# Windowed attention and two MLP layers on one core: the later plain pairs take q, scores and v another way, and ScalarE adds the 1e-9

## The chip, the core and the metric

The kernel runs on one core of a Trainium2 chip. The metric is the device time of one launch in microseconds; the median of three runs before the change is 904.41 us (902.61 to 905.0). The engines are TensorE (PE in the profile, its weight loads PEld), VectorE (DVE), ScalarE (ACT), GpSimd (POOL) and SyncE (SP), which here only issues DMAs.

## What is computed

Four batches of eight heads, 576 positions, 64 elements a head. Heads 0 to 3 are plain (a window of 32 positions back), heads 4 to 7 dilated (32 positions, each fourth one). Two MLP layers follow on the 2304 tokens.

```python
scores = scale * np.matmul(q, k.transpose(0, 1, 3, 2))
mask_plain = (rel >= 0) & (rel < window)
mask_dil = (rel >= 0) & (rel < window * dilation) & (rel % dilation == 0)
...
scores = np.where(masks[None, :, :, :], scores, -1000000000.0)
scores = scores - np.max(scores, axis=-1, keepdims=True)
attn = np.exp(scores)
attn = attn / (np.sum(attn, axis=-1, keepdims=True) + 1e-09)
return np.matmul(attn, v).astype(np.float32)
...
h = x @ w_in
g = np.maximum(0.01 * h, h)
return (g @ w_out).astype(np.float32)
...
h = x @ w_in
g = np.maximum(h, 0.0) + np.log1p(np.exp(-np.abs(h)))
return (g @ w_out).astype(np.float32)
```

## The kernel before

**Attention.** The tokens fall into eight windows of 288 (half a batch each, `w` 0 to 7), and in each window the heads into four pairs (`p` 0 to 3; 0 and 1 plain, 2 and 3 dilated): 32 pairs. A plain pair's window is cut into three tiles of 96 queries with 128 keys each, a dilated one into four of 72 queries, one for each residue. Scores stand with the keys in the partitions. The pairs of windows 0 and 1 are early: q and k are loaded in rows, transposed by TensorE, and the two heads' scores come as separate matmuls on 64 partitions each (`scores_early`, L603). The others are late: SP loads q and k in blocks of 32 by 32 (`load`, L523), VectorE transposes the blocks (`trans_k` L578, `trans_q` L585), and `trans_q` writes each head's q into its own half of a tile `qz` whose other half is zero, so that one matmul on 128 partitions gives the scores of both heads (`scores`, L630). VectorE adds the mask on the way out of PSUM (`mask`, L644), POOL takes the maximum over the partitions (`rowmax`, L654), VectorE subtracts it (L658), ScalarE takes the exponential (L661).

**Products with v.** In most pairs the exponentials are the stationary operand and v with a column of ones the moving one, so that the sums come along (`pv`, L679); VectorE adds 1e-9 to the sums, inverts them and multiplies (`inv`, L689 to L691), TensorE transposes the result (`xT`, L700). The dilated pairs from window 3 on (`turned`) keep v stationary: `pv_late` (L710) gives the result transposed at once, POOL sums the exponentials over the partitions (`sums`, L718), VectorE spreads, inverts and multiplies (L726 to L738). Both ways end in x, split into a high part by ScalarE (L757) and a low one by VectorE (L761).

**The MLPs.** Layer 1 takes the tokens in blocks (256, 256, 352, then 288 each) and the hidden units in 16 pieces `f`; a step is twelve matmuls `h` (L783), activation and split on ScalarE (L799, L804) and VectorE (`gl`, L808), and two steps later twelve matmuls `yp` (L826). Each of these stretches of twelve is called a group here. The first two blocks run interleaved. Layer 1's weights are converted ahead of the first products (low part by VectorE, L378). Layer 2's weights are converted piece by piece during layer 1 (L318 to L363) and stored to DRAM; layer 2 runs behind layer 1 with nothing of attention beside it. In the first 60 us, matmuls on constants (`spin`, L453) fill TensorE's idle time.

**What sets the order.** Every operation is an `Op` with an engine, an assumed cost, what it needs and frees, and a due time; `run_schedule` plays them through on assumed clocks and writes out one order for each engine. The engines then run in that order and wait for each other by semaphores. So a changed cost or due time anywhere can move rows on every engine. `C2A` and `C2B` set when layer 2's pieces are due; layer 1's chain of groups is fixed, and attention's work is put between the groups.

## Time and profile before

| | |
|---|---|
| runs, median (lowest to highest) | 904.41 us (902.61 to 905.0) |
| profiled execution, its own time | 903.69 us |
| its span, first to last instruction | 901.9 us |
| mean granted TensorE clock | 0.989 of full |
| busy PE, DVE, ACT, POOL | 98%, 71%, 44%, 13% |
| first product of layer 1 | 44.52 us |
| last of attention's low parts of x ends | 457.47 us |

The span is cut at the first and last instruction; a profile's times are from the span's start. A busy share is an average over stages with different limits: the first 60 us, layer 1 with attention between its groups (to about 505 us) and layer 2 are three of them. One matmul of 32-bit floats in attention shows as two records, and records overlap, so what a block costs is read from the starts of the matmuls ahead of it and behind it.

### The profile page before, as it was taken

To read this page: it belongs to the slowest core of one execution; us is meant where nothing else is said; L and a number is where in the kernel's file an instruction comes from. 1 tells how busy PE (TensorE), PEld (TensorE's weight loads), DVE (VectorE), ACT (ScalarE), POOL (GpSimd) and SP (SyncE) were. 2 spreads that over 40 slices of the span, in tenths; PEclk is the share of its full clock that TensorE was granted. 3 is DMA by queue.
4 is the path that set the end of the run, shared out by engine and by line. 5 is a ranking of instruction groups with operands and counts; after the bars stand their busy time and mean duration, and the time that the engine had idled before them with its cause. 6 is when DMAs were issued, how large, how long until landed. Compare 5 with 4: busy or idle time off the path is not lost.

```text
span 901.9 us, 16361 instructions
## 1 busy us (share of the span) xinstructions
PE 882.0 (98%) x6391; PEld 831.8 (92%) x6392; DVE 640.5 (71%) x1165; ACT 397.3 (44%) x763; POOL 112.8 (13%) x67
## 2 busy tenths in 40 slices
PE   6989999999999999999999999999999999999998
PEld 4879999999999999999999999988888888888886
DVE  3989996588688787786853675766765776576663
ACT  3767764444445444444435653323422432243231
POOL 5400021032042240221400000000000000000000
PEclk9879999999999999999999999999999999999999
DMA  9879124554565546554248477433443352325332
GB/s 237 220 212 312 21 36 98 168 133 120 139 176 173 139 124 173 156 156 158 72 148 292 136 222 236 149 94 101 162 143 109 112 170 94 107 104 156 103 94 93
DMA packets 157985, 131.89 MB, mean 146 GB/s; under 512 B 102100, under 2 KB 138964, under 8 KB 157908
## 3 DMA queue, kind: packets, MB, share of 16 engines
q1 hardware_dynamic: 155508, 130.26, 48.8%
q8 instruction: 50, 0.82, 0.4%
q10 hardware_dynamic: 2400, 0.59, 0.4%
q14 instruction: 27, 0.22, 0.1%
HBM read 104.60 MB, written 26.21 MB: 145 GB/s over the span
## 4 chain that ended last, share of the span: by engine, by line
PE 93%; DVE 1%; DMA 1%; ACT 0%; SPq 0%; issue 0%; DVEq 0%
PE yo L1032 22%; PE h L783 22%; PE yp L826 22%; PE h L959 17%; PE sc L630 3%; PE hp L1020 2%; PE pv L679 2%; PE pv L710 1%; PE xt L700 1%; DMA w2s<-cs 1%; DMA raw<-in_moe_w_out_dram 0%; PE sc L603 0%; DVE cf L336 0%; SPq L523 0%; DVE lent L658 0%
## 5 line engine op out<-in xcount | busy, mean ns | idle before, releaser
L783 PE MATMUL h<-xh,w 128*128 128x288 f32 (+2 forms) x1024 | 231.3, 301 | 1.2 <-DVE w L378 1.2
L826 PE MATMUL yp<-gh,w 128*128 128x288 f32 (+2 forms) x1024 | 229.4, 299 | 1.0 <-DVE ys L836 0.9
L1032 PE MATMUL yo<-wo,w 128*128 128x512 f32 x864 | 222.9, 395 | 0.0
L959 PEld LDWEIGHTS h<-tr,w 128*128 128x128 f32 x1344 | 174.3, 188 | 11.1
L1032 PEld LDWEIGHTS yo<-wo,w 128*128 128x128 f32 x864 | 152.5, 188 | 27.1
L959 PE MATMUL h<-tr,w 128*128 128x256 f32 x1344 | 176.7, 279 | 0.0
L783 PEld LDWEIGHTS h<-xh,w 128*128 128x128 f32 x1024 | 173.0, 190 | 1.9 <-DVE w L378 1.4
L826 PEld LDWEIGHTS yp<-gh,w 128*128 128x128 f32 x1024 | 171.7, 188 | 1.7 <-DVE ys L836 1.5
L783 PE MATMUL h<-xl,w 128*128 128x288 f32 (+2 forms) x512 | 152.0, 297 | 0.0
L826 PE MATMUL yp<-gl,w 128*128 128x288 f32 (+2 forms) x512 | 150.9, 295 | 0.0
L799 ACT ACTIVATE hc<-h 128x288 f32<-128x288 f32 (+2 forms) x128 | 52.4, 410 | 162.0 <-PE h L783 160.2
L997 ACT ACTIVATE ex<-ex 128x512 f32<-128x512 f32 x72 | 45.5, 632 | 154.8 <-DVE ex L994 154.7
L808 DVE TENSOR_TENSOR gl<-hc,gh 128x288 fp32r<-128x288 f32 (+2 forms) x128 | 68.0, 532 | 41.9 <-ACT gh L804 40.8
L783 PEld LDWEIGHTS h<-xl,w 128*128 128x128 f32 x512 | 97.3, 190 | 0.0
L826 PEld LDWEIGHTS yp<-gl,w 128*128 128x128 f32 x512 | 96.3, 188 | 0.2
L654 POOL PARTITION_ALL_REDUCE mx<-s x24 | 50.6, 2107 | 297.7 <-DVE s L644 294.0
L1000 DVE SCALAR_TENSOR_TENSOR ex<-hs,ex 128x512 f32<-128x512 f32 x64 | 44.3, 692 | 34.7 <-ACT ex L997 34.0
L1005 ACT ACTIVATE w<-ex 128x512 fp32r<-128x512 f32 x72 | 45.3, 629 | 33.0 <-DVE ex L1000 33.0
L804 ACT ACTIVATE gh<-hc 128x288 fp32r<-128x288 f32 (+2 forms) x128 | 56.6, 443 | 2.9
L1009 DVE TENSOR_TENSOR w<-ex,w 128x512 fp32r<-128x512 f32 x72 | 49.8, 691 | 11.5 <-ACT w L1005 6.5
L318 ACT ACTIVATE cf<-raw 128x512 f32<-128x512 f32 (+1 forms) x48 | 39.8, 830 | 22.4 <-DMA raw<-in_moe_w_out_dram 9.7
L336 DVE CUSTOM_DVE_ANT_0 cf<-raw,cf 128x1024 uint16<-128x1024 uint16 (+1 forms) x48 | 44.8, 933 | 1.0
(103 smaller groups left out, 964.7 us busy)
## 6 DMA issues: line engine op xcount, KB each, us to landing
wo<-w2o SPq DMA_DIRECT2D x80, 512.0 KB
raw<-in_moe_w_in_dram SPq DMA_DIRECT2D x32, 512.0 KB
raw<-in_moe_w_out_dram SPq DMA_DIRECT2D x32, 512.0 KB
w2o<-cf SPq DMA_DIRECT2D x16, 512.0 KB
out_dram<-o SPq DMA_DIRECT2D x36, 128.0 KB
w2a<-cf SPq DMA_DIRECT2D x8, 512.0 KB
w2s<-cs SPq DMA_DIRECT2D x8, 512.0 KB
w<-w2a SPq DMA_DIRECT2D x8, 512.0 KB
```

What stands on the lines that cost most here:

```text
L336: nc.vector.tensor_tensor(out=self.cf, in0=self.cf, in1=self.raw[:, :, 0], op=ALU.add)
L654: nc.gpsimd.partition_all_reduce(self.mx, self.sf, channels=P, reduce_op=bass_isa.ReduceOp.max)
L783: nc.tensor.matmul(out=h, lhsT=a[:, c, :], rhs=b_[:, c, :], start=(c == 0 and a is whi and b_ is xh), stop=(c == NC - 1 and a is wlo))
L799: nc.scalar.activation(out=hc, in_=hbank.pop(s), func=AF.Prelu, alpha=0.01)
L804: nc.scalar.activation(out=gh, in_=hcopy[s], func=AF.Copy)
L808: eng.tensor_sub(out=gl, in0=hcopy.pop(s), in1=gparts[s][0].bitcast(F32))
L826: nc.tensor.matmul(out=ybank[e][:, o:o + n], lhsT=a[:, e * P:(e + 1) * P], rhs=b_, start=(f == 0 and n == unit_len[u] and a is whi and b_ ...
L959: nc.tensor.matmul(out=bank[m, b][:, half], lhsT=w[:, a, kb * P:(kb + 1) * P], rhs=t[:, b_, kb], start=(kb == 0 and a + b_ == 0), stop=(kb ...
L997: nc.scalar.activation(out=self.ex, in_=self.ex, func=AF.Softplus)
L1005: nc.scalar.activation(out=self.gh, in_=self.ex, func=AF.Copy)
L1009: nc.vector.tensor_sub(out=self.gl, in0=self.ex, in1=self.gh.bitcast(F32))
L1032: nc.tensor.matmul(out=obank[c, t], lhsT=a, rhs=b_, start=(opens and n == 0), stop=(closes and n == 2))
```

## The change

Four things are changed, and the planner's numbers with them.

- Plain late pairs: `trans_q` transposes q in place, both heads in one instruction on 128 partitions, and `scores_plain` takes six matmuls on 64 partitions each, the heads alternating between the two halves, into two PSUM tiles; `mask_plain` masks head by head, with the masks in 16 bits.
- The sum of 1e-9 is made by ScalarE (`inv_sum`), for all pairs that are not turned; `inv` then only inverts and multiplies.
- The first pair (`p` 0) of windows 4 to 7 is turned: v stays stationary, POOL sums.
- The due times of layer 2's pieces: 110 us and 14 us a piece up to the sixth, then 26 us a piece, where it was 125 us and 19.9 us a piece throughout.

```diff
-            self.turned = w >= TURN and self.dil
+            self.turned = w >= TURN and (self.dil or w > TURN and p == 0)
...
         def trans_q(self):
+            if not self.dil:
+                self.qt = self.qr.rearrange("x n p -> x (n p)")
+                nc.vector.transpose(out=self.qt, in_=self.qr)
+                return
...
+        def scores_plain(self):
+            m = self.m
+            self.s = att.tile([P, self.nt, 2, m], F32, tag="s", name="s")
+            self.sc = [ps_a.tile([P, self.nt, m], F32, tag="at", name="sc") for j in range(2)]
+            for i in range(self.nt):
+                for j in range(2):
+                    hd = slice(D * j, D * j + D)
+                    nc.tensor.matmul(
+                        out=self.sc[j][:, i],
+                        lhsT=self.kt[hd, self.step * i:self.step * i + P],
+                        rhs=self.qt[hd, m * i:m * i + m],
+                        start=True, stop=True)
+
+        def mask_plain(self, j):
+            mk = masks_b if self.first else masks_b[:, 1:2].to_broadcast([P, self.nt, self.m])
+            nc.vector.tensor_tensor(out=self.s[:, :, j], in0=self.sc[j], in1=mk, op=ALU.add)
...
+        def inv_sum(self, half):
+            t0, t1, ps = self.po[half]
+            n, m = t1 - t0, self.m
+            self.rd[half] = rd = att.tile([m, n, 2, 1], F32, tag="rd", name="rd")
+            nc.scalar.activation(out=rd, in_=ps[:, :, :, D:D + 1], func=AF.Identity, bias=tiny[0:m])
...
-            rd = att.tile([m, n, 2, 1], F32, tag="rd", name="rd")
-            nc.vector.tensor_scalar_add(out=rd, in0=ps[:, :, :, D:D + 1], scalar1=1e-9)
+            rd = self.rd[half]
             nc.vector.reciprocal(out=rd, in_=rd)
...
-    C2A, C2B = 125.0, 19.9
+    C2A, C2B, C2N, C2C = 110.0, 14.0, 6, 26.0
...
-                tq = [Op("dve", 1.0 if turned else 1.2, a.trans_q, deps=[a.lq] + old_kq, rel=["qr"], lock=LOCKT, **m)]
+                tq = [Op("dve", (1.0 if turned else 1.2) if dil else 0.48, a.trans_q, deps=[a.lq] + (old_kq if dil else []),
+                         rel=["qr"] if dil else [], lock=LOCKT, **m)]
...
+            elif not dil:
+                a.o_s1 = Op("pe", 0.84, a.scores_plain, deps=[tk] + tq, acq=["at", "at", tag_s], rel=["qr"],
+                            order=[prev(1, "o_s1")], **ms)
+                cs = [Op("dve", dve(3 * a.m, True), a.mask_plain, j, deps=[a.o_s1], rel=["at"], hold=hold, **m) for j in range(2)]
...
-                norms.append(Op("dve", 0.8 if dil else 0.95, a.inv, half, deps=[pv],
-                                acq=["rd"], rel=[a.room(half if dil else p)[1], "rd"], **m))
+                sm = Op("act", 0.2, a.inv_sum, half, deps=[pv], acq=["rd"], **m)
+                norms.append(Op("dve", 0.63 if dil else 0.78, a.inv, half, deps=[sm],
+                                rel=[a.room(half if dil else p)[1], "rd"], **m))
...
-        c2 = C2A + C2B * (f + (which or 0) / 2)
+        c2 = f + (which or 0) / 2
+        c2 = C2A + C2B * min(c2, C2N) + C2C * max(c2 - C2N, 0.0)
```

**Where rows move.** First VectorE in the first 35 us, before the change: the third and fourth of the early pairs' subtractions of the maximum (`lent`), the first two normalisations (`rd`, `xn`) and the next step of a layer-1 piece (`cp`, L323).

```order
L658 TENSOR_TENSOR lent<-lent 128x576
L689 TENSOR_SCALAR rd<-pv 96x6
L690 RECIPROCAL rd<-rd 96x6
L691 TENSOR_TENSOR xn<-pv,rd 96x384
L658 TENSOR_TENSOR lent<-lent 128x576
L689 TENSOR_SCALAR rd<-pv 96x6
L690 RECIPROCAL rd<-rd 96x6
L691 TENSOR_TENSOR xn<-pv,rd 96x384
L323 TENSOR_SCALAR cp<-cf 128x1024
```

The same place on VectorE in the change:

```order
L677 TENSOR_TENSOR lent<-lent 128x576
L714 RECIPROCAL rd<-rd 96x6
L715 TENSOR_TENSOR xn<-pv,rd 96x384
L677 TENSOR_TENSOR lent<-lent 128x576
L714 RECIPROCAL rd<-rd 96x6
L715 TENSOR_TENSOR xn<-pv,rd 96x384
L677 TENSOR_TENSOR lent<-lent 128x576
L323 TENSOR_SCALAR cp<-cf 128x1024
```

The adds are gone, and the fifth subtraction stands ahead of the layer-1 piece. ScalarE at that place in the change (`lent<-sc` copies scores out, `lent<-lent` is the exponential, `rd<-pv,warm` the new sum, `cf<-raw` the second layer-1 piece's first step):

```order
L569 ACTIVATE lent<-tr 128x288
L708 ACTIVATE rd<-pv,warm 96x6
L622 ACTIVATE lent<-sc 128x288 x2
L680 ACTIVATE lent<-lent 128x576
L708 ACTIVATE rd<-pv,warm 96x6
L318 ACTIVATE cf<-raw 128x1024
```

Before, `cf<-raw` stood right behind the first of these rows; it is now behind two sums, two copies and an exponential. In the stretch up to the end of the early pairs TensorE also has 51 matmuls on constants where it had 42.

Second, TensorE in window 4 before the change: the first pair's products with v and the second pair's scores.

```order
L826 MATMUL yp_3028<-gh,w 128x288
L679 MATMUL pv<-v_94,s 96x65 x6
L630 MATMUL sc<-qz_91,kt_93 128x192 x2
L783 MATMUL h<-xh,w 128x288
...
L783 MATMUL h<-xh,w 128x288
L630 MATMUL sc<-qz_91,kt_93 128x192
L700 MATMUL xt<-ident,xn 128x96 x3
L826 MATMUL yp_3005<-gh,w 128x288
```

In the change the first pair's products are these, and the second pair's scores follow four groups later in one block of six:

```order
L734 MATMUL pv<-s,v_95 64x96 x6
L850 MATMUL yp_3062<-gh,w 128x288
...
L807 MATMUL h<-xh,w 128x288
L648 MATMUL sc<-qr,kt_94 128x96 x6
L850 MATMUL yp_3062<-gh,w 128x288
```

The transposes of that pair are gone. Counted in groups of twelve, the last pair's products with v of windows 4, 5, 6 and 7 stand at groups 123, 155, 187 and 219, before the change at 122, 154, 186 and 216; the next block of layer 1 begins behind groups 126, 158, 190 and 222 in both.

Third, VectorE where layer 1 goes from its second to its third block (`gl` is the low part of a step's activations, the others are layer 2's conversion, `ys` copies out of PSUM), before the change:

```order
L808 TENSOR_TENSOR gl<-hc,gh 128x256
L323 TENSOR_SCALAR cp<-cf 128x512
L327 SCALAR_TENSOR_TENSOR cf<-cf,cp 128x512
L336 ISA cf<-raw,cf 128x1024
L808 TENSOR_TENSOR gl<-hc,gh 128x256 x2
L808 TENSOR_TENSOR gl<-hc,gh 128x352
```

The same place in the change:

```order
L832 TENSOR_TENSOR gl<-hc,gh 128x256
L323 TENSOR_SCALAR cp<-cf 128x512
L327 SCALAR_TENSOR_TENSOR cf<-cf,cp 128x512
L336 ISA cf<-raw,cf 128x1024
L346 TENSOR_TENSOR cs<-cf 128x256
L832 TENSOR_TENSOR gl<-hc,gh 128x256
L346 TENSOR_TENSOR cs<-cs,cf 128x256
L346 TENSOR_TENSOR cs<-cf 128x256
L346 TENSOR_TENSOR cs<-cf,cs 128x256
L832 TENSOR_TENSOR gl<-hc,gh 128x352
```

A piece's sums (L346), which came some five steps later, stand here now. Between the 30th and the 52nd `gl` four pieces' last step (L363) stood before, seven do now; from there on they are about seven steps apart.

## Rows read from the trace of the kernel before

**Rows 1.** The page, part 1: busy us, share of the span, instructions.

```profile
PE 882.0 (98%) x6391; PEld 831.8 (92%) x6392; DVE 640.5 (71%) x1165; ACT 397.3 (44%) x763; POOL 112.8 (13%) x67
```

**Rows 2.** Windows of 10 us: length, busy PE, PEld, DVE, ACT, POOL, clock, DMA, GB/s.

```profile
40.00:50.00 10.00, 8.15 (x89) 7.13 (x86) 9.59 (x21) 7.01 (x17) 2.96 (x2) 1.00 0.60 129
50.00:60.00 10.00, 7.90 (x43) 7.69 (x44) 7.55 (x18) 7.83 (x12) 0.00 (x0) 0.50 0.67 163
...
150.00:160.00 10.00, 10.00 (x79) 10.00 (x79) 2.60 (x7) 4.09 (x10) 0.00 (x0) 1.00 0.38 84
...
210.00:220.00 10.00, 10.00 (x75) 9.70 (x74) 9.09 (x17) 3.41 (x7) 4.25 (x2) 1.00 0.30 85
```

**Rows 3.** Timeline of TensorE: start, duration, then idle before and its releaser.

```profile
48.03 1.58 PE L679 MATMUL pv<-lent 104*72 104x65 f32 x16 [1.61 <-ACT lent L661]
...
51.08 0.80 PE L783 MATMUL h<-xh,w 128*128 128x256 f32 x2 [1.19 <-DVE w L378]
...
234.11 0.40 PE L826 MATMUL yp<-gh,w 128*128 128x288 f32 x1 [0.94 <-DVE ys L836]
```

**Rows 4.** The chain that ended last, two groups: start, duration.

```profile
56.30 2.67 PE h L783 x12
...
62.72 1.40 PE h L783 x12
```

**Rows 5.** Timeline of TensorE around a plain pair's products and transposes (window 5).

```profile
362.43 0.29 PE L783 MATMUL h<-xh,w 128*128 128x288 f32 x1
362.56 1.15 PE L679 MATMUL pv<-v,s 128*96 128x65 f32 x12
...
363.74 0.29 PE L826 MATMUL yp<-gl,w 128*128 128x288 f32 x1
...
367.00 0.30 PE L783 MATMUL h<-xh,w 128*128 128x288 f32 x1
367.13 0.41 PE L700 MATMUL xt<-ident,xn 96*128 96x96 f32 x3
...
367.54 0.29 PE L826 MATMUL yp<-gl,w 128*128 128x288 f32 x1
```

**Rows 6.** Timeline of TensorE around a plain pair's scores, undivided.

```profile
353.06 0.29 PE L826 MATMUL yp<-gh,w 128*128 128x288 f32 x1
353.19 1.14 PE L630 MATMUL sc<-qz,kt 128*128 128x192 f32 x6
...
354.30 0.29 PE L826 MATMUL yp<-gl,w 128*128 128x288 f32 x1
```

**Rows 7.** Timeline of TensorE around a dilated pair's products, v stationary.

```profile
276.42 0.29 PE L826 MATMUL yp<-gh,w 128*128 128x288 f32 x1
276.64 0.72 PE L710 MATMUL pv<-s,v 104*64 104x72 f32 x16
...
277.53 0.30 PE L783 MATMUL h<-xl,w 128*128 128x288 f32 x1
```

**Rows 8.** Timeline of TensorE around an early plain pair's scores.

```profile
25.26 0.91 PE L603 MATMUL sc<-lent 64*128 64x96 f32 x12
26.10 0.54 PE L453 MATMUL spin<-masksb,identb 128*128 128x288 bf16 x3
```

**Rows 9.** Groups by line and form: busy us, mean ns, idle before.

```profile
L585 DVE STREAM_TRANSPOSE qz<-qr 64x288 f32<-64x288 f32 x48 | 28.4, 592 | 0.7
...
L689 DVE TENSOR_SCALAR rd<-pv 96x6 f32<-96x6 f32 x16 | 2.5, 157 | 5.3 <-PE pv L679 5.2
...
L757 ACT ACTIVATE xh<-xt 128x64 fp32r<-128x64 f32 x4 | 0.9, 216 | 0.0
```

**Rows 10.** Timeline of VectorE, then TensorE, where window 4's x is wanted.

```profile
281.49 0.69 DVE L761 TENSOR_TENSOR xl<-xn,xh 128x288 fp32r<-128x288 f32 x1
...
282.20 0.30 PE L826 MATMUL yp<-gh,w 128*128 128x288 f32 x1
...
283.80 0.30 PE L783 MATMUL h<-xh,w 128*128 128x288 f32 x1
```

More of the change, by code (lines that the diff above doesn't have):

```diff
@@ L387 @@
     masks_b = attp.tile([P, NI, QP], BF16, tag="masksb", name="masksb")
+    tiny = attp.tile([P, 1], F32, tag="warm", name="warm")
     zero = attp.tile([P, 1], BF16, tag="zero", name="zero")
@@ L435, in warm_up @@
     def warm_up():
-        t = attp.tile([P, 1], F32, tag="warm", name="warm")
         nc.gpsimd.partition_all_reduce(
-            t, ident[:, 0:1], channels=P, reduce_op=bass_isa.ReduceOp.max)
+            tiny, ident[:, 0:1], channels=P, reduce_op=bass_isa.ReduceOp.max)
+        nc.gpsimd.memset(tiny, 1e-9)
     BLOCKS = [(0, 256), (256, 256), (512, 352)] + [(t, T1) for t in range(3 * T1, NT, T1)]
@@ L638, in mask @@
             n, m = t1 - t0, self.m
-            if self.first and not self.dil and half == 0:
-                mk = masks[:, 0:2]
-            else:
-                sel = 0 if (self.first and self.dil) else 1
-                mk = masks[:, sel:sel + 1, 0:m].to_broadcast([P, n, m])
+            sel = 0 if self.first else 1
+            mk = masks[:, sel:sel + 1, 0:m].to_broadcast([P, n, m])
             nc.vector.tensor_tensor(
@@ L672, in pv @@
                 self.xn = att.tile([m, self.nt, 2, D], F32, tag="xn", name="xn")
-                self.po = {}
+                self.po, self.rd = {}, {}
             pool, tag = self.room(half if self.dil else self.p)
@@ L1180 @@
                         y_free[2 * (p % 2) + j].append(cs[j])
+            elif not dil:
+                a.o_s1 = Op("pe", 0.84, a.scores_plain, deps=[tk] + tq, acq=["at", "at", tag_s], rel=["qr"],
+                            order=[prev(1, "o_s1")], **ms)
+                cs = [Op("dve", dve(3 * a.m, True), a.mask_plain, j, deps=[a.o_s1], rel=["at"], hold=hold, **m) for j in range(2)]
             else:
-                blk = 0.33 if not dil else 0.29 if w < TURN else 0.2
+                blk = 0.29 if w < TURN else 0.2
                 s0 = Op("pe", 2 * blk, a.scores, 0, deps=[tk] + tq, acq=["at", tag_s],
```

## The prediction

> **What bounds the kernel now.** I read the page's shares first: TensorE is busy 98% of the span [rows 1]. Then the busy time by stretches of 10 us: from 60 us on TensorE has no idle time worth naming, while VectorE swings between 2.60 us of 10 (150 to 160) and 9.09 (210 to 220) [rows 2]. Then I went through TensorE's timeline from 62 us on and looked for steps between two matmuls longer than usual. Beside the attention blocks I found one real wait, 0.94 us at 234 us for a VectorE copy out of PSUM [rows 3]. So from 62 us on time is what TensorE has to do, and an edit pays by what it takes off TensorE, or costs by a wait that it makes there. Ahead of 62 us the picture is another: TensorE waits for the exponentials and for the converted weights (1.61 and 1.19 us) [rows 3], VectorE is at 9.59 of 10 from 40 to 50 us, and from 50 to 60 us the granted clock is 0.50, the lower level of 1.2 GHz, behind those waits [rows 2]. There VectorE's chain bounds, and the clock doubles what TensorE does: a group of twelve products takes 2.67 us at 56 us and 1.40 us at 63 us [rows 4].
>
> **What the blocks cost now.** An ordinary step is (283.80 - 282.20) / 12 = 0.133 us [rows 10]. The price of a block put into this stream is the distance from the last matmul ahead of it to the second behind it, less two steps of 0.133; the second, since the first behind a block often stands longer. A plain pair's products with v: 363.74 - 362.43 - 0.27 = 1.04 us; its three transposes: 367.54 - 367.00 - 0.27 = 0.27 [rows 5]. Scores of a plain pair: 354.30 - 353.06 - 0.27 = 0.97 [rows 6]. A dilated pair with v stationary (16 records of 72 columns): 277.53 - 276.42 - 0.27 = 0.84 [rows 7].
>
> **Change, part by part.**
>
> v stationary in four plain pairs (windows 4 to 7, first pair). Removed from TensorE: 1.04 + 0.27 = 1.31 us each. Added: 12 records of 96 columns. By records they cost 12/16 of 0.84 = 0.63, by columns (12 x 96 against 16 x 72, equal) 0.84. I take the middle, 0.74: gain 0.57 each, **2.3 us** for four (1.9 to 2.7).
>
> Scores in halves of the rows, twelve later plain pairs. The early pairs do this already, with the same twelve records of 64 rows and 96 columns: 26.10 - 25.26 = 0.84 us from their start to the next block's [rows 8]. What a change to halves costs on entry shows in the column halves: 276.64 - 276.42 = 0.22 where a step is 0.133, so 0.09 [rows 7]. The block then costs 0.84 to 0.93; I take 0.89 against 0.97: **1.0 us** for twelve (0.5 to 1.6). The masks stay 576 elements a pair. The Trainium skill, TensorEngine Tiling (Array Packing), Theoretical Speedup, gives up to twofold for a contraction of 64. By that rule the part would come to 5.8 us; the early pairs' blocks do not agree with it (0.84 for the records that would then take 0.49).
>
> q transposed in place: one instruction of 288 in place of two of 592 ns each [rows 9]; it was timed on 64 partitions, and the count of elements in a partition is unchanged. Twelve times 0.59 is 7.1 us off VectorE. Behind 62 us VectorE ends one wait of TensorE, so I price it at nothing; if VectorE is what is late (rival 4) it is relief. The q buffer is now held until the scores are done, so a later q load waits longer in SP's queue, and with it the k and v loads and layer-2 pieces behind; there are two such buffers, no wait of TensorE goes back to a load of q, and I take nothing.
>
> 1e-9 on ScalarE: 28 VectorE adds of about 0.157 us [rows 9] leave before, 24 small ScalarE operations come, and four pairs go to the other path, which has its own add. A ScalarE operation on 6 elements is not in the trace: under the 0.216 of 64 elements [rows 9], and I put it above the 0.157 of VectorE; take 0.2. Eight of the adds stand ahead of the second pair of layer-1 weights on VectorE, the instruction that the 1.19 us wait was for: 8 x 0.157 = 1.2 us earlier at best. ScalarE is in order and was at 7.01 of 10 there [rows 2], so a sum that waits for its products now holds back the exponentials and weight copies queued behind it, 8 x 0.2 = 1.6 us at worst. TensorE also gets nine more of the idle-time matmuls (51 for 42), 9 x 0.133 = 1.2 us if they meet real work. The new path is one engine longer, products, ScalarE, VectorE, but the step changes place with one of about its length. I take **0.8 us** gained, bounds 2.0 gained (1.2, and half of the 1.27 by which the group at 56 us is slower than the one at 63) and 2.8 lost (1.6 and 1.2).
>
> Four more sum reductions on POOL, and the longer VectorE tail of that path in place of the short one: TensorE does not wait for POOL anywhere behind 62 us, and what VectorE gets here is less than the sums and transposes take off it. Nothing, as long as VectorE keeps up (rival 4).
>
> The later x. In window 4 the last pair's x is done at 281.49 + 0.69 = 282.18 and TensorE wants it at 283.80: 1.62 us to spare [rows 10]. In the new order that pair's products with v stand three groups of twelve ahead of the wanted step, before it was four, and a group is 1.60 us; in windows 5 and 6 the same, in window 7 three for six. If the chain behind the products keeps its length, the spare time is zero. I charge **0.4 us** in all, bounds 0 and 3 (0.7 at each of four edges).
>
> Conversion dates of layer 2. Seven in place of four pieces end between the 30th and the 52nd step of layer 1, then they thin out. They fall where VectorE had 7.4 us of 10 free (150 to 160) and where it had 0.9 (210 to 220) [rows 2]. The one wait of 0.94 us there may go or get company: nothing, with 0.9 either way. The last piece's store comes later by one or two steps of layer 1, with some thirteen steps left; nothing.
>
> **The sum.** -2.3 - 1.0 - 0.8 + 0.4 = -3.7 us. The profiled execution took 903.69 us (span 901.9 and 1.8 around it), which lies inside the three runs (902.61 to 905.0) and 0.7 under their median. From the one 900.0, from the other 900.7: I say 900.5. A change of under 0.3%, 2.7 us, can hardly be told from none here.
>
> **The rivals.**
>
> 1. The forecast, 900.5, own range 898.8 to 902.3. For it: no waits to hide behind from 62 us on. Chance 0.50, of which 0.40 under 901.7.
>
> 2. What TensorE saves it waits away: x arrives late at the edges of the four blocks behind windows 4 to 7 (0.7 us each), so 2.8 of the 3.7 go: 903.3. For it: spare time near zero. Against: a place in the order counts whole groups, so up to a group of the shift may be rounding. Chance 0.17.
>
> 3. The change of halves costs on both sides of twelve blocks. By rows: 0.84 + 0.09 on entry + 0.13 for the longer first step behind a block (rows 6 hold one, 0.97 against 0.84) = 1.06, which is 0.09 more than now, 1.1 us lost where 1.0 was gained: 902.6. The Trainium skill, TensorEngine Tiling (Array Packing), Key Properties, states that changing the tiling mode drains TensorE; by that rule this is the case that comes. The 0.22 us entry agrees in kind. Chance 0.07.
>
> 4. Slower: layer-2 conversions crowd VectorE between 190 and 260 us, and the low parts of layer 1's activations come late behind them. Each such wait costs what the one at 234 us did, 0.94 [rows 3]. From four of them on the gain is gone, with seven it is 900.5 + 6.6 = 907. For it: 9.09 of 10 before any is added. Against: 0.59 us a plain pair and 0.157 a sum leave VectorE [rows 9], and a low part has two steps until it is used. Chance 0.13.
>
> 5. Better: TensorE keeps 2.4 GHz in the start-up, since the nine added idle-time matmuls sit where it waited. Two groups at 2.67 become 1.40: 2.5 us more, and no wait at the edges (0.4): 897.6. Against: the waits of 1 to 2 us that came ahead of the fall stay in kind. Chance 0.11. Halves that overlap fully would make a block of scores half of 0.97, 5.8 us off in place of 1.0, 895.7; against it stand the 0.84 us of the early blocks [rows 8]. Chance 0.02.
>
> **From cases to numbers.** Faster by over 0.3%: 0.40 + 0.13 = 0.53. Within: 0.10 + 0.17 + 0.07 = 0.34. Slower: 0.13. The range from 896.8 to 905.2 takes in the bounds of the terms and leaves out most of case 4 and the full overlap, under 0.2.
>
> **What would show it.** Right: the plain block with v stationary inserted at 0.6 to 0.85 us and no transposes in those pairs; the halved scores at 0.84 to 0.93; the second weights' low part some 1 us ahead of 51 us; no new waits of TensorE behind 62 us. Wrong: waits of TensorE on x at the first product of a block or on the copies out of PSUM; a stretch at clock 0.50 longer than 10 us ahead of 62 us; halved scores over 1.0 us.

## The result and the profile after

The changed kernel takes 908.28 us (median of 20 runs, 903.77 to 919.5) where the kernel before takes 903.11 in the same session (20 runs, 901.76 to 905.0). The ratio is 1.0062, with an interval of 1.004 to 1.0084: slower, by more than 0.3%, where I had said 900.5 and a range up to 905.2. One run, the 919.5, fell into a disturbed state and is left out of the ratio. The profiled execution took 904.88 us, with a span of 902.7, so it is one of the shorter ones.

The page of the changed kernel, part 1, answers to [rows 1]: TensorE is as busy as before, VectorE is less so.

```profile
PE 883.3 (98%) x6460; PEld 827.0 (92%) x6461; DVE 628.6 (70%) x1141; ACT 399.6 (44%) x787; POOL 126.0 (14%) x72
```

What changed is the chain that ended last (part 4). In the kernel before it is 93% TensorE, 1% DMA and 1% VectorE.

```profile
PE 88%; DMA 5%; DVE 4%; issue 1%; ACT 1%; SPq 1%; POOL 0%; ACTq 0%; DVEq 0%
```

The windows of the changed kernel answer to [rows 2], with two more.

```profile
40.00:50.00 10.00, 7.99 (x87) 7.05 (x86) 9.44 (x17) 7.80 (x17) 3.15 (x2) 1.00 1.01 237
50.00:60.00 10.00, 8.82 (x67) 8.12 (x67) 9.36 (x20) 8.24 (x15) 0.00 (x0) 0.83 0.54 103
150.00:160.00 10.00, 10.00 (x77) 10.00 (x76) 4.37 (x10) 5.20 (x11) 0.00 (x0) 1.00 0.78 251
160.00:170.00 10.00, 9.42 (x65) 8.81 (x64) 8.47 (x15) 3.45 (x8) 1.96 (x1) 1.00 0.70 220
180.00:190.00 10.00, 7.87 (x59) 7.51 (x58) 3.92 (x8) 4.59 (x10) 0.00 (x0) 1.00 0.74 244
210.00:220.00 10.00, 10.00 (x75) 9.70 (x74) 9.48 (x16) 4.22 (x8) 5.28 (x2) 1.00 0.22 62
```

From 180 to 190 us TensorE lacks 2.13 us, and VectorE is busy for only 3.92 us of the ten. So VectorE is not crowded there; it waits itself. TensorE's waits of the changed kernel from 80 us on are these (total, times, longest), where the kernel before has the 0.94 us of [rows 3] alone (one more, new as well, lies ahead of 80 us: 1.27 us at 62.77 for a low part of x; it comes back in the part on the 1e-9 below):

```profile
PE sc L648 <- ACT gh L828: 2.1, 1, 2.1
PE yp L850 <- DVE ys L860: 2.0, 2, 1.4
```

VectorE's waits between 100 and 260 us for the store of `cs` (2.7, once, in the kernel before):

```profile
DVE cp L323 <- DMA w2s<-cs: 10.6, 3, 5.1
```

The timelines of VectorE, ScalarE, SyncE's queue and TensorE in the changed kernel tell how the 2.13 us came about.

```profile
179.82 0.52 DVE L832 TENSOR_TENSOR gl<-hc,gh 128x352 fp32r<-128x352 f32 x1
185.48 0.43 DVE L323 TENSOR_SCALAR cp<-cf 128x512 uint32<-128x512 uint32 x1 [5.14 <-DMA w2s<-cs]
...
188.14 0.69 DVE L363 TENSOR_TENSOR cf<-cf 128x512 fp32r<-128x512 f32 x1 [0.26 <-ACT cf L360]
188.75 0.18 DVE L714 RECIPROCAL rd<-rd 96x6 f32<-96x6 f32 x1
189.03 0.55 DVE L715 TENSOR_TENSOR xn<-pv,rd 96x384 f32<-96x384 f32 x1
```

```profile
182.91 0.67 ACT L318 ACTIVATE cf<-raw 128x512 f32<-128x512 f32 x1 [3.45 <-DMA raw<-in_moe_w_out_dram]
...
187.48 0.63 ACT L360 ACTIVATE cf<-cf 128x512 fp32r<-128x512 f32 x1 [2.47 <-DVE cf L336]
188.02 0.25 ACT L708 ACTIVATE rd<-pv,warm 96x6 f32<-96x6 f32 x1
```

```profile
179.93 0.33 SPq L356 DMA_DIRECT2D w2s<-cs  x1
```

```profile
182.11 1.15 PE L698 MATMUL pv<-v,s 128*96 128x65 f32 x12
...
187.09 0.46 PE L648 MATMUL sc<-qr,kt 64*128 64x96 f32 x2
189.69 0.88 PE L648 MATMUL sc<-qr,kt 64*128 64x96 f32 x10 [2.13 <-ACT gh L828]
```

Read it from the store. `cs`, the column sums of a pair of layer-2 pieces, lies in the same single buffer as `cp`, the shifted word of the next piece. The store of `cs` is issued at 179.93, and VectorE's next instruction in order wants that buffer: it stands from 180.34 to 185.48. Not all of this is the store's: the instruction also reads `cf`, the piece's first step on ScalarE, which waited for the piece's load and ended only at 183.58. The last 1.9 us are the store's alone. The conversion then runs late, ScalarE stands 2.47 us for it, and behind that stands the new 1e-9 step of a plain pair whose products with v were done at 183.3. The reciprocal and the product that free that pair's PSUM bank end at 189.58, and at 189.69 TensorE, which needs a second bank for the halved scores, goes on. The profile names ScalarE's `gh` as the releaser, since it ended at the same time (189.55); the bank fits the order better, and the record of TensorE's sequencer that waits there on VectorE's semaphore (and on a DMA's) ends at 189.63. The two waits on `ys`, which end at 162.24 and 236.95, come behind such stands too:

```profile
159.71 0.43 DVE L323 TENSOR_SCALAR cp<-cf 128x512 uint32<-128x512 uint32 x1 [2.62 <-DMA w2s<-cs]
...
227.79 0.43 DVE L323 TENSOR_SCALAR cp<-cf 128x512 uint32<-128x512 uint32 x1 [2.86 <-DMA w2s<-cs]
...
236.03 0.43 DVE L323 TENSOR_SCALAR cp<-cf 128x512 uint32<-128x512 uint32 x1 [2.98 <-ACT cf L318]
```

The second of them has one more link. Just ahead of it VectorE stood 2.98 us for ScalarE, and ScalarE 3.11 us until 235.34 for another store, that of a converted piece (`w2o`) out of the buffer `cf`, which the late conversion had finished only at 231.65.

**A ledger.** TensorE's products of layer 1 come in stretches, `h` and `yp` in turn. I number them and take the start of the 27th (97.14 us in the kernel before) and of the 251st (510.37). What a kernel gains or loses by the 27th I call the start, from there to the 251st the middle; behind the 251st all kernels agree within 0.07 us. In the first profile of the changed kernel the start is 1.83 us earlier (95.31) and the middle 2.66 longer (511.20 - 95.31 - 413.23).

### The profile page after: what moved, and what is told of

It reads as the page before. It is cut to its first block, busy times and chain, and to the rows that moved or that the text cites. A ratio compares the mean times of both kernels' runs of the same rounds, so it can differ in the third digit from the quotient of the medians.

```text
span 902.7 us, 16564 instructions
## 1 busy us (share of the span) xinstructions
PE 883.3 (98%) x6460; PEld 827.0 (92%) x6461; DVE 628.6 (70%) x1141; ACT 399.6 (44%) x787; POOL 126.0 (14%) x72
## 4 chain that ended last, share of the span: by engine, by line
PE 88%; DMA 5%; DVE 4%; issue 1%; ACT 1%; SPq 1%; POOL 0%; ACTq 0%; DVEq 0%
PE yo L1056 22%; PE yp L850 20%; PE h L807 19%; PE h L983 17%; PE hp L1044 2%; PE pv L698 2%; DMA w2s<-cs 2%; PE sc L635 1%; DVE cf L327 1%; PE sc L648 1%; DMA raw<-in_moe_w_out_dram 1%; PE pv L734 1%; DMA rows<-in_k_dram 1%; DVE cf L336 1%; PE sc L608 1%
## 5 line engine op out<-in xcount | busy, mean ns | idle before, releaser
L807 PE MATMUL h<-xh,w 128*128 128x288 f32 (+2 forms) x1024 | 228.2, 298 | 1.2 <-DVE w L378 1.2
L742 POOL PARTITION_ALL_REDUCE sm<-s x14 | 52.3, 3733 | 27.4 <-ACT s L680 27.4
```

Source lines behind the costliest of these rows:

```text
L742: nc.gpsimd.partition_all_reduce(self.sm, self.sf, channels=P, reduce_op=bass_isa.ReduceOp.add)
L807: nc.tensor.matmul(out=h, lhsT=a[:, c, :], rhs=b_[:, c, :], start=(c == 0 and a is whi and b_ is xh), stop=(c == NC - 1 and a is wlo))
```

## The experiments

The experiments are numbered 1 to 18; "run 9" is the ninth and "kernel 9" its kernel. Two things stood out beside the waits: the runs of the changed kernel spread over 13 us (903.77 to 917.02), and its idle-time matmuls begin at 3.14 us where they began at 8.50, which I call the early start. VectorE's second cast of the masks is what they wait for; it stands like this in the changed kernel, and then in the kernel before.

```profile
2.89 0.20 DVE L431 CAST masksb<-masks 128x96 bf16<-128x96 f32 x1
```

```profile
2.89 5.55 DVE L430 CAST masksb<-masks 128x96 bf16<-128x96 f32 x1
```

In the kernel before POOL's row of memsets starts at 2.89 with the cast; in the changed one the new memset of 1e-9, which starts at 3.08 us, holds that row back until the cast has gone. The Trainium skill, SBUF — State Buffer, section SBUF: two separate sides, says that VectorE, in some of its modes, and GpSimd share a pair of ports under an exclusive lock, and that the one that starts first holds it for the whole instruction. The rows agree with a lock of that kind (no run shows the mode of the cast), and here the cast lost not one instruction but a row of them.

| kernel | start of stretch 27 | stretch 251 | middle, against before | TensorE's waits from 80 us | median | ratio, interval |
|---|---|---|---|---|---|---|
| before | 97.14 | 510.37 | 0 | 0.9 | 903.11 | |
| changed | 95.31 | 511.20 | +2.66 | 4.1 | 908.28 | 1.0062, 1.004 to 1.0084 |
| 1 changed again | 103.08 | 519.70 | +3.39 | 3.3 | 907.62 | 1.005, 1.0022 to 1.0078 |
| 2 late start | 97.27 | 515.97 | +5.47 | 3.9 | 908.16 | 1.0052, 1.0029 to 1.0074 |
| 3 before, early start | 98.66 | 511.83 | -0.06 | 0.9 | 903.65 | 1.0006, 0.9988 to 1.0024 |
| 4 old dates | 94.72 | 508.65 | +0.70 | 2.5 | 902.9 | 1.0009, 0.9982 to 1.0035 |
| 5 dates alone | 96.51 | 512.51 | +2.77 | 3.0 | 906.45 | 1.0032, 1.0008 to 1.0057 |
| 6 halves alone | 95.30 | 515.32 | +6.79 | 4.6 | 909.3 | 1.0061, 1.0042 to 1.0079 |
| 7 v stationary alone | 95.50 | 509.32 | +0.59 | 2.7 | 905.36 | 1.0014, 0.9996 to 1.0032 |
| 8 old dates, filled wait | 99.02 | 512.66 | +0.41 | 1.4 | 904.34 | 1.0004, 0.9987 to 1.0021 |
| 9 own buffer | 101.35 | 512.35 | -2.23 | 0 | 904.37 | 1.0012, 0.999 to 1.0033 |
| 10 old dates, own buffer | 103.81 | 516.75 | -0.29 | 1.7 | 904.36 | 1.0028, 1.0 to 1.0057 |
| 11 old dates, VectorE adds | 99.55 | 522.75 | +9.97 | 8.0 | 911.92 | 1.0109, 1.0089 to 1.0129 |
| 12 before, v stationary, own buffer | 96.85 | 507.70 | -2.38 | 0.5 | 900.94 | 0.9973, 0.9964 to 0.9983 |
| 13 changed, own buffer, late start | 93.58 | 504.67 | -2.14 | 0 | 898.5 | 0.9954, 0.9931 to 0.9978 |
| 14 before, own buffer | 97.03 | 509.82 | -0.44 | 0.6 | 901.96 | 0.9972, 0.9946 to 0.9998 |
| 15 halves, own buffer | 102.75 | 523.12 | +7.14 | 4.9 | 908.61 | 1.0064, 1.0041 to 1.0086 |
| 16 as 12, and sums on ScalarE | 93.27 | 504.63 | -1.87 | 0.5 | 900.28 | 0.9958, 0.9939 to 0.9977 |
| 17 as 13, full-row scores | 97.37 | 514.39 | +3.79 | 5.5 | 905.14 | 1.0025, 1.001 to 1.0041 |
| 18 late start again | 93.93 | 511.54 | +4.38 | 4.2 | 908.0 | 1.0051, 1.0032 to 1.0071 |

The times of stretches 27 and 251 and the waits are those of the one profiled execution of each; the ratio is to the kernel before in the same session, whose median went from 902.55 to 903.53 between sessions, so kernels of different sessions are better compared by their ratios.

**1. The changed kernel again**, no edit.

> The changed kernel as it is, once more, to have its spread and a second profile on the chip of the next three. Theory A (start-up): a time around 908 us whose runs differ by several us, each longer run with a lower mean granted clock, and in the profile a stretch at granted clock 0.50 between 15 and 60 us whose length makes up the difference to the first profile (904.88 us, some 17 us at 0.50). Theory B (waits between 160 and 240 us): around 908, and the difference to the kernel before stands in TensorE's waits behind 160 us.

The spread is there: 904.78 to 916.08. Its profiled run is 8.5 us longer than the first (span 911.2, mean granted clock 0.978 for 0.990), and 7.8 us of it is the start. Windows of this run:

```profile
20.00:30.00 10.00, 9.98 (x63) 8.13 (x63) 4.03 (x6) 4.18 (x12) 1.96 (x1) 0.50 0.60 130
30.00:40.00 10.00, 10.00 (x69) 8.90 (x69) 4.44 (x11) 6.61 (x16) 3.93 (x2) 0.50 0.94 286
40.00:50.00 10.00, 9.83 (x70) 8.08 (x71) 4.93 (x10) 4.59 (x11) 1.96 (x1) 0.59 0.97 249
```

At the lower level of 1.2 GHz from 20 us to past 40, where the first profile was back at 0.93 from 30 to 40. So most of what differs between these two is how long the start runs at half clock. The middle differs by 0.7 us, with a granted clock of 0.98 from 160 to 260 us where the first profile has 1.00.

**2 and 18. The late start alone**, the same kernel twice.

```diff
+        nc.vector.memset(tiny, 1e-9)
...
-        nc.gpsimd.memset(tiny, 1e-9)
```

> The changed kernel, but the 1e-9 is set by VectorE in the set-up and not by POOL behind its first all-reduce, so that POOL's row of long memsets follows the all-reduce at once, as in the kernel before. Theory A: VectorE's cast of the masks again takes some 5.5 us beside those memsets, the idle-time matmuls start near 8.5 and not near 3.1 us, the transposes near 13.9 and not 8.7, TensorE no longer runs into the loads of k and q (2.4 us at 15.7), and the median comes down from about 908 to about 904.5, with runs within 3 us. Theory B: the start-up is not what costs; about 908.

> The changed kernel with the late start alone, a second time: 908.2 before, where the late start took 5.9 us off the kernel without waits behind the store (904.4 to 898.5). If the late start's gain is eaten by the wait of 2.2 us at 188 us with a stretch of half clock behind it (0.91 from 160 to 200 us in the first profile), the second profile shows that stretch again and the median is 907 to 909. If the first 12 runs were an accident of the start-up, it is 903 to 905, some 5 us above the kernel with both edits.

The cast took 5.55 us again, the transposes began at 14.38 and 13.75 us, and the medians stayed at 908. The start did get better by the second profile (93.93), but the middle got worse: with the wait of 2.1 us at 188 us comes a stretch of half clock. From 160 to 200 us, in run 2 and then in run 18:

```profile
160.00:200.00 40.00, 37.46 (x235) 36.26 (x234) 24.37 (x45) 16.62 (x35) 4.05 (x2) 0.91 0.64 189
```

```profile
160.00:200.00 40.00, 37.24 (x241) 36.11 (x240) 26.91 (x51) 17.24 (x35) 6.01 (x3) 0.96 0.64 183
```

The first profile of the changed kernel has 1.00 there. What the clock takes, 9% and 4% of 40 us, is 3.6 and 1.6 us, near what these two middles lose beyond that of the first profile (2.8 and 1.7). So the start alone was not the cause, and a wait can cost more than its length.

**3. The kernel before with the early start alone.**

```diff
             t, ident[:, 0:1], channels=P, reduce_op=bass_isa.ReduceOp.max)
+        nc.gpsimd.memset(t, 1e-9)
```

> The kernel before, with one small POOL memset behind its first all-reduce and nothing else (its value is used by nothing). Theory A: the cast of the masks takes 0.2 us in place of 5.55, the idle-time matmuls start near 3.1 us, and the median rises from 903.1 to about 906.5, with runs spread over 5 us or more. Theory B: 903.1, within 0.2%, since the head start is lost again by 45 us and nothing else is touched.

903.65, no difference that can be told: theory A, alone, fell. The transposes begin 5.5 us earlier (8.34 for 13.87), and the head start is gone by the 27th stretch. It goes as half clock: the mean granted clock of these 12 runs is 0.982 to 0.987, that of the kernel before in the session mostly 0.99 and more.

**4. The changed kernel with the old dates.**

```diff
-    C2A, C2B, C2N, C2C = 110.0, 14.0, 6, 26.0
+    C2A, C2B, C2N, C2C = 125.0, 19.9, 6, 19.9
```

> The changed kernel with the conversion dates of layer 2 as in the kernel before (125 us and 19.9 us a step throughout). Theory A: about 908, as the changed kernel, since the start-up is untouched. Theory B in its form that the dates crowd VectorE between 160 and 240 us: the 4.4 us that the changed kernel loses there against the kernel before go, and it comes to about 904. If the loss there comes from the scores' blocks and the longer path of the plain pairs with v stationary, the waits stay though the dates are back, and it stays near 908.

902.9: theory B. The wait at 188 us is gone, others of 1.1 and 1.4 us remain. VectorE still waits for stores of `cs`, 11.3 us in seven from 80 to 520 us against 10.9 in four with the new dates: with the old dates they fall elsewhere and cost TensorE less.

**5. The dates alone** in the kernel before (the new numbers and the formula that uses them).

> The kernel before with the new conversion dates of layer 2 (110, 14 a step to the sixth piece, 26 behind it) and nothing else. Theory C, the dates alone crowd VectorE: TensorE waits some 3 to 4 us more than the kernel before between 160 and 260 us, and the median is 906.5 to 908. Theory D, the dates do harm only beside the plain pairs' other edits (longer path through ScalarE, blocks of scores in two banks): no new wait there, 903.2 within 0.15%.

Theory C: 906.45 and 2.77 us lost in the middle, by these waits of TensorE.

```profile
PE yp L826 <- DVE ys L836: 3.0, 3, 1.8
```

VectorE's stands ahead of the two longer ones (TensorE 1.08 us until 163.16 and 1.75 us until 236.93):

```profile
160.62 0.43 DVE L323 TENSOR_SCALAR cp<-cf 128x512 uint32<-128x512 uint32 x1 [4.08 <-DMA w2s<-cs]
...
236.35 0.52 DVE L836 COPY ys<-yp 128x352 f32<-128x352 f32 x1 [2.90 <-DMA y<-ys]
```

The first is the store of `cs`, the second and longer one a store of y out of its staging buffer. Whether the own buffer of run 9 would take this second one away too was not run for the dates alone.

**6. The halves alone**: `scores_plain`, `mask_plain` and the q transpose in place put into the kernel before.

> The kernel before with the scores of the twelve later plain pairs in halves of the rows and q transposed in place, and nothing else. By the blocks of the changed kernel (1.03 against 0.97 us) it loses 0.06 us each, 0.7 in all: 903.9, with the same waits of TensorE as the kernel before. By the price of my prediction (0.89) it gains 1.0: 902.2. If the relief of VectorE by 7.1 us counts on the path, it gains more, and the wait of 0.94 us at 234 us goes.

909.3, and 6.79 us in the middle, ten times the loss by the blocks. The new order has waits of its own. VectorE, then TensorE:

```profile
356.55 0.46 DVE L857 COPY ys<-yp 128x288 f32<-128x288 f32 x1 [1.75 <-DMA y<-ys]
```

```profile
357.07 0.40 PE L847 MATMUL yp<-gh,w 128*128 128x288 f32 x1 [1.48 <-DVE ys L857]
```

The copy of y out of PSUM waits until an earlier store of y has left its staging buffer: a store again, of another buffer. The clock is 0.78 from 355 to 360 us behind it.

**7. v stationary alone.**

```diff
-            self.turned = w >= TURN and self.dil
+            self.turned = w >= TURN and (self.dil or w > TURN and p == 0)
```

> The kernel before with v stationary in the first plain pair of windows 4 to 7, and nothing else (dates, sums and scores as before). By the blocks of the changed kernel (0.84 us for 1.31) it gains 4 x 0.47 = 1.9: 901.4. If x comes late at the edges of the four blocks behind, the gain is gone: 903.2 or more, and TensorE waits on x at the first product of a block.

905.36, which its interval does not tell from the kernel before, and waits of 2.7 us on `ys`: the gain of 1.9 is eaten, though not by x.

**8. The start's wait filled**, on kernel 4.

```diff
+    FILLW = 3.2
...
-                        ls.append(Op("bw", 1.1 if w == 0 else 1.4, lambda: None, deps=[o], **m))
+                        ls.append(Op("bw", 1.1 if w == 0 else FILLW, lambda: None, deps=[o], **m))
```

> The changed kernel with the conversion dates of before, and with 3.2 us in place of 1.4 as the time that the planner gives the second window's rows of k and q to land, so that 9 idle-time matmuls stand where TensorE waited 2.4 us for these rows at 15.7 us. If the half-clock stretch of the start-up comes from that wait, the granted clock between 18 and 32 us is 1.00 and the profiled span is 3 to 5 us under that of the kernel with the old dates alone (900.2): 896 to 897, with a median of 898 to 900. If the clock falls at the next wait just the same, the span stays near 900 and the median near 903.

No gain: 904.34. The windows of 10 us show that the clock holds up to 20 us (1.00 for 0.96 in kernel 4) and falls a little later (0.67 for 0.53).

```profile
10.00:20.00 10.00, 9.58 (x106) 7.27 (x104) 4.47 (x3) 7.29 (x17) 6.21 (x5) 1.00 1.09 313
20.00:30.00 10.00, 7.97 (x49) 6.67 (x50) 7.47 (x10) 5.22 (x12) 3.27 (x2) 0.67 0.57 126
```

The runs lie closer together (902.67 to 906.0, kernel 4 900.93 to 910.34).

**9. An own buffer for the shift.** For layer 2 the shifted word goes into the half of the raw tile that is already read; order and dates stay.

```diff
-            self.cp = wraw.tile([P, self.n], U32, tag="cp", name="cp", bufs=1)
+            if self.layer:
+                self.cp = self.raw[:, :, 1]
+            else:
+                self.cp = wraw.tile([P, self.n], U32, tag="cp", name="cp", bufs=1)
```

> The changed kernel, order and dates untouched, but the shifted word of a layer-2 piece (cp) is written into the half of the piece's raw tile that is already read, and no longer into the buffer that it shares with the column sums (cs), which stays taken until their store has landed. Theory E (VectorE's queue stands behind that store: 2.6, 5.1 and 2.9 us idle at 157, 180 and 225 us, and TensorE's waits of 0.6, 2.1 and 1.4 us at 161, 188 and 234 us each follow one): those idle times of VectorE go, TensorE's waits behind 100 us fall from 4.1 us to under 1, and from 100 to 260 us the kernel gains some 1 us on the kernel before in place of losing 2.9; the median falls by 3 to 4.5 us to 903.5 to 905. Theory F (VectorE has simply too much work at the new dates): the waits stay within 1 us of what they were, and the median with them, 907 to 908; the strided write of 512 words can even cost 0.25 us a piece.

This is the run that decides. VectorE's waits for the store, 10.6 us between 100 and 260 us, are gone, and so is every wait of TensorE from 80 us on; the middle goes from +2.66 to -2.23. VectorE does the same work in the same order at the same dates (the shifted word takes 0.43 us as before), so theory F falls. VectorE does not stop waiting: in place of the store it now waits for the piece's first step on ScalarE, 7.3 us in five where it was 3.2 in two, and at the place of the 5.14 us it still stands 2.34. But that is 2.8 us less, and TensorE's 2.13 us are gone.

```profile
187.55 0.43 DVE L326 TENSOR_SCALAR raw<-cf 128x512 uint32<-128x512 uint32 x1 [2.34 <-ACT cf L318]
```

The windows from 160 us:

```profile
160.00:200.00 40.00, 40.00 (x278) 39.35 (x277) 27.16 (x50) 20.72 (x42) 4.89 (x3) 1.00 0.72 218
200.00:260.00 60.00, 60.00 (x458) 58.58 (x457) 49.01 (x97) 26.18 (x55) 18.62 (x8) 1.00 0.52 151
```

The median of 904.37 is 3.9 us under the changed kernel's; its runs go from 899.03 to 908.29 (four up to 901.53 with a mean granted clock of 0.990, eight from 903.92 on with 0.979 to 0.984), and the profiled one, of the eight, began its 27th stretch at 101.35 us. That is the start.

**10. The own buffer at the old dates.**

> The same edit of the buffer on the changed kernel with the conversion dates of before. Theory E: the waits of VectorE for the store (2.8 and 3.5 us at 221 and 344 us, 8.7 in six) go too, and TensorE's two waits of 1.1 and 1.4 us with them: 2 us under the kernel with the old dates alone, a median of 900.5 to 901.5 and a profiled span of 897.5 to 899. Theory F: within 0.5 us of it, 902.9.

A miss in the median (904.36; the profiled run reached its 27th stretch of products at 103.81 only); in the middle it gains 0.99 on kernel 4. Its two waits shrank to 1.0 and 0.7 us and did not go, so at the old dates the store is not their only head.

**11. VectorE's adds at the old dates**: kernel 4 without `inv_sum`.

> The changed kernel with the conversion dates of before and 1e-9 added by VectorE again, to show what the step on ScalarE does. By my prediction the start-up loses its 0.8 us: the group of products that begins at 60.2 us in the kernel with the old dates begins about 0.8 us later, and the median is some 0.8 above 902.9. If the ScalarE step costs because it queues behind exponentials and weight copies, the start-up is up to 1.6 us earlier, and the wait of 1.1 us on xn goes.

Far outside both expectations: 911.92. Leaving 24 small steps on VectorE re-plans the whole order, and three waits of the kind of run 5 come, one of 4.2 us with half clock behind it (0.94 from 200 to 260 us).

```profile
PE yp L851 <- DVE ys L861: 7.1, 3, 4.2
```

It tells nothing of the start.

**12. The kernel before with v stationary and the own buffer.**

> The kernel before with two things alone: v stationary in the four plain pairs, and the layer-2 shift written into the raw tile. Theory E: TensorE's waits behind 100 us, 2.7 us with v stationary alone, fall under 0.7, and what v stationary takes off TensorE (1.9) shows: between 100 us and the end 1.5 to 2.5 us less than the kernel before, a median of 900.5 to 902. Theory F: as v stationary alone, 905.4, with the waits of 2.7 us.

900.94: theory E, and faster than the kernel before. Against run 7, the middle goes from +0.59 to -2.38. What v stationary gives shows in the middle (-2.38 for run 14's -0.44, the buffer alone); the ratios of the two do not tell it (0.9973 and 0.9972).

```profile
PE yp L829 <- DVE ys L839: 0.5, 2, 0.3
```

**13. Both: own buffer and late start**, on the changed kernel (the edits of 9 and 2).

> The changed kernel with two edits: the layer-2 shift written into the raw tile, and the 1e-9 set by VectorE so that POOL's memsets follow the all-reduce at once, as before. If the median of the changed kernel is made of the waits behind the store (4.9 us between 100 us and the end by the ledger of the products' groups) and of the early start's half-clock time, this takes both away: about 900.9, runs within 4 us of each other, mean granted clock 0.990 or more. If the early start does not matter, it is as the kernel with the buffer edit alone, 904.4 with runs over 9 us.

898.5, the fastest kernel of the study, 0.46% under the kernel before and 1.1% under the changed one. Seven of its runs lie at 897.56 to 898.57 and five at 901.88 to 902.87 with a lower mean granted clock, so the median could have come out some 3 us higher. No wait of TensorE from 80 us on:

```profile
160.00:200.00 40.00, 40.00 (x279) 39.33 (x278) 29.07 (x52) 18.28 (x39) 9.62 (x4) 1.00 0.65 179
200.00:260.00 60.00, 60.00 (x474) 58.36 (x473) 48.04 (x94) 27.29 (x58) 19.34 (x7) 1.00 0.55 157
```

**14. The kernel before with the own buffer.**

> The kernel before with the layer-2 shift written into the raw tile and nothing else: the control for the next two. By theory E the one wait of 0.94 us at 234 us goes, and with it 0.9 us: 901.7 against 902.6. If the wait was VectorE's own work, it stays, and the time too.

As expected: 901.96, and the wait of [rows 3] at 234 us is gone. It was a wait for the store too: VectorE had stood 2.68 us until 228.67. A new one of 0.6 us came at a pair's products.

**15. The halves with the own buffer.**

> The kernel before with the halved scores and q in place, and the layer-2 shift written into the raw tile: the price of the halves without the waits behind the store. By blocks of 1.03 for 0.97 us it is 0.7 above the kernel before with the buffer edit alone, some 902.4. If other waits come with it (two score banks held at once in place of one after the other), it is 905 or more and TensorE waits at sc or pv.

908.61: the second case of the expectation. 4.9 us of waits stay, on `ys` above all; the buffer that helps elsewhere does nothing for this order.

**16. Kernel 12 with the sums on ScalarE.**

> The kernel before with v stationary in four plain pairs, the buffer edit and the 1e-9 on ScalarE: against the same without the ScalarE step (900.94). By my prediction's term the start-up gains 0.8 us: 900.1. By its bounds 898.9 to 903.7; if the step queues behind ScalarE's exponentials and weight copies the group of products that begins at 65 us begins later by up to 2.8 us.

900.28, 0.66 under kernel 12, near the 0.8 predicted, but of another session, and the intervals of the two ratios overlap: not shown. In the two profiles the start is 3.6 us earlier (93.27 for 96.85), and nearly all of it is the clock from 50 to 60 us (0.85 for 0.51); TensorE's wait for the second weights ends 0.47 us earlier (49.64 for 50.11).

**17. Kernel 13 with the scores over the full rows.**

> The fastest kernel so far (the changed kernel with the buffer edit and the late start, 898.5), but the scores of the later plain pairs over the full rows again, with q transposed into zero-padded tiles. By the blocks it gains 12 x 0.06 = 0.7: 897.8. If the halves are what brings new waits (as they did alone), or their relief of VectorE matters, it shows as waits of TensorE behind 100 us in one of the two kernels and a difference above 1 us.

6.6 us slower. The two views of waits (TensorE, VectorE) show why.

```profile
PE yp L853 <- DVE ys L863: 5.5, 4, 2.1
```

```profile
DVE ys L863 <- DMA y<-ys: 9.3, 4, 3.7
```

So here it is stores of y that hold the staging buffer, in an order that this edit alone brought about. Hence the halves themselves cannot be priced by taking them out; their blocks can (below).

## Why the prediction was wrong

**The step that failed** is "Conversion dates of layer 2 ... The one wait of 0.94 us there may go or get company: nothing, with 0.9 either way." I had put their waits at nothing, and in the changed kernel TensorE's waits grew from 0.94 to 4.1 us; with the old dates its median is back at 902.9 (run 4). Alone the dates cost 2.8 us in the middle (run 5), though there the longest wait comes behind a store of y. I had looked at how much time VectorE has free at the new dates, and it has enough: with its own buffer it does the same work at these dates without one wait of TensorE (run 9). What it lacked was the buffer, which a store held for 5.6 us from its issue (179.93 to 185.48), the last 1.9 of them with nothing else in the way, and with everything queued behind the one instruction that wanted it. The trace of before held it, and I stopped at the VectorE copy that [rows 3] names for the 0.94 us. VectorE's timeline there:

```profile
228.67 0.43 DVE L323 TENSOR_SCALAR cp<-cf 128x512 uint32<-128x512 uint32 x1 [2.68 <-DMA w2s<-cs]
```

The failed step carries over 3 us of the 5.6 by which the middle missed (2.9 gained was said, 2.66 lost came); the halved scores carry 1.7 more, the rest is small or open.

**Rival 4** (slower, 907, chance 0.13) named the right edit and came nearest, by another mechanism: not crowded but standing, 3.92 us busy of ten in the worst window.

**v stationary**: sized a little high. The block stands in the changed kernel at 305.53 - 304.43 - 0.27 = 0.83 us (all four 0.83 to 0.84) where I took 0.74: what it costs goes by columns, not by records. 0.48 gained each, 1.9 for 2.3, at the low bound. Timeline of TensorE, this block and the halved scores:

```profile
304.43 0.29 PE L807 MATMUL h<-xh,w 128*128 128x288 f32 x1
304.65 0.72 PE L734 MATMUL pv<-s,v 128*64 128x96 f32 x12
...
305.53 0.29 PE L850 MATMUL yp<-gl,w 128*128 128x288 f32 x1
...
311.66 0.29 PE L807 MATMUL h<-xh,w 128*128 128x288 f32 x1
311.88 0.91 PE L648 MATMUL sc<-qr,kt 64*128 64x96 f32 x12
312.73 0.40 PE L850 MATMUL yp<-gh,w 128*128 128x288 f32 x1
312.96 0.29 PE L850 MATMUL yp<-gl,w 128*128 128x288 f32 x1
```

**Halved scores**: wrong sign. 312.96 - 311.66 - 0.27 = 1.03 us (1.03 to 1.05 in the ten of the twelve blocks on which no wait falls) for 0.97, so 12 x 0.06 = 0.7 lost where I had 1.0 gained. The mis-sized term is the 0.84 from the early pairs: it ends at the first matmul behind the block, while the 0.97 holds the longer first step behind it. Measured alike, from a block's first matmul to the first behind, the halves take 312.73 - 311.88 = 0.85 us and the full rows in the kernel before 354.03 - 353.19 = 0.84:

```profile
354.03 0.43 PE L826 MATMUL yp<-gh,w 128*128 128x288 f32 x1
```

So the halves themselves gain nothing, and the entry costs 0.22 us where a step is 0.133. Rival 3 came near in its price (1.06) and was right in the entry; the longer first step, 312.96 - 312.73 = 0.23 us, is no cost of the halves, for the full rows have it too (354.30 - 354.03 = 0.27). I gave that case 0.07. The Trainium skill, TensorEngine Tiling (Array Packing), Key Properties, says that changing the tiling mode drains TensorE; the rows agree with it on entry and show nothing of it on leaving.

**The ledger closes with these two.** -1.9 + 0.7 - 0.94 (the old wait) = -2.1; kernels 13 and 9, without a wait, have -2.14 and -2.23. In the changed kernel the waits add 4.1: +2.0 of the measured 2.66; the remaining 0.7 is not accounted for.

**The later x**: 0.4 charged, nothing came; no wait on x stands at the edges behind windows 4 to 7. The wait on x that did come is another, in the start (below). The transposes of q: nothing, as said, as far as this can be seen.

**1e-9 on ScalarE**: 0.8 gained is not shown. Run 16 lies near it (0.66 under run 12 in the medians), within the noise, and the sign that I had named did not come: TensorE's wait for the second weights ends at 51.78 us in the changed kernel, later than the 51.08 of [rows 3]. The new order also brought a wait for a low part of x, which stands at 61 to 71 us in all eleven profiles of the table with the sums on ScalarE (0.28 to 1.35 us) and in none of the nine without. In the changed kernel:

```profile
62.77 0.38 PE L807 MATMUL h<-xl,w 128*128 128x256 f32 x1 [1.27 <-DVE xl L785]
```

And I had not looked at where the constant of that step is made. Its memset changed who comes first, VectorE's cast or POOL's memsets, and moved the start of the idle-time matmuls by 5 us. Alone this does nothing (run 3); with the waits gone, undoing it gives 5.9 us in the medians, 5.2 by the ratios (13 against 9).

**What stays open.** The changed kernel's median lies 3.4 us above its first profile. In run 1 most of the excess is half clock in the start; of the other runs only the mean granted clock is known, which falls from 0.99 in the short ones to 0.976 in the long ones. My sign for a bad start, a stretch at clock 0.50 of over 10 us ahead of 62 us, came in both profiles. Why a start takes one course or another from run to run no experiment here tells. The middle can be told to about 1 us from one profile (the same kernel twice: 2.66 and 3.39, 5.47 and 4.38), the start only from many runs. Whether the early start costs in general is open too: over 5 us between 9 and 13, nothing between the kernel before and 3. But it does go with a lower clock: no run in the seven rows of the table with the early start has a mean granted clock above 0.993, while of the rows with the late one all but row 11 have runs at 0.995 and more.

## What to carry to other kernels

When a kernel has one wait left, follow it to its head: the engine that is named as the releaser may itself have stood behind a DMA, and what then moves (dates, an order) lands on that. In a kernel whose order is planned as a whole, price an edit by the waits of the new order and not by the work that it takes away: in the middle, 1.9 us of less work became 0.6 us lost (run 7), and came back as soon as one buffer was no longer shared with a store (run 12). A buffer that a store empties should not be the one that the next instruction of an in-order queue writes.

## What the runs showed of the hardware

A cast of 96 columns took 5.55 us beside a row of POOL memsets and 0.20 us ahead of it, at the same start of 2.89 us: the order of two small instructions on two engines moves the beginning of TensorE's work by over 5 us. A wait of some 2 us in the full stream can be followed by 1.2 GHz (0.91 and 0.96 over 40 us in runs 2 and 18, 1.00 in the first profile of the changed kernel, with the same wait). Six matmuls over 64 rows (twelve records) cost 1.03 us in the stream where three over the full rows (six records), half of them zeros, cost 0.97; between first matmul and first behind both take 0.84 to 0.85, and the entry is 0.22 us for 0.13. An instruction of VectorE that writes a buffer under a store of 512 KB stood until 5.0 to 5.9 us behind the store's issue.
